# A table that overrides single decisions of a list scheduler, in an attention and feed-forward kernel

## The chip, the cores and the metric

The kernel runs on one core of a Trainium2 chip. The metric is device time in microseconds (us), the median of several runs. Before the change it is 757.0 us, the median of three (756.21, 757.00, 758.24). The profile shown is of one execution with a span of 754.6 us.

## The reference

One transformer block on x of 2048 rows and 512 columns, bf16: a layer norm, attention with 32 heads of width 16 and no mask, a residual, a second layer norm, and a gated feed-forward block of width 1792.

```python
qkv = layernorm(x) @ wqkv                    # 32 heads, Dh = 16
scores = einsum("bhqd,bhkd->bhqk", q, k) * 16 ** -0.5
h = x + einsum("bhqk,bhkd->bhqd", softmax(scores), v) @ wo
n = layernorm(h)
out = h + (sigmoid(n @ w_gate) * (n @ w_up)) @ w_down
```

The size that matters is the number of exponentials: 32 heads of 2048 x 2048 scores, 134 million.

## The kernel before, in words

**Units and rounds.** The work on the scores is cut into units. A unit is 128 keys by 512 queries of one head, or 256 keys by 256 queries in two halves; either way it fills one bank of PSUM, the matmul accumulator memory, as 128 x 512. Units go in *rounds*, numbered from 0, 695 of them. A round takes two or, for most of the kernel, three units. TensorE (PE) writes their scores (line 1085). ScalarE (ACT) takes the exponential of two or three neighbouring units in a single instruction (line 1408) and writes it as fp16 to *slots* in SBUF, the on-chip memory. The last unit of a round can go to VectorE (DVE) instead: a *split*. There the exponential is approximated by a sum of three pieces: VectorE makes an integer word (line 1256, tile J), GpSimd (POOL) makes two shifted copies of it by 64-bit additions (line 1277), and all three are multiplied with the values. So a unit on VectorE needs three value matmuls where a unit on ScalarE needs one. GpSimd or VectorE work is done for two such units at a time, and six buffers hold those pairs.

**Value rows.** Line 1233 multiplies the exponentials with V, augmented by a column that sums them. The output of a head has only 17 rows, so four heads (the strips j = 0 to 3 of a group) share the PE array side by side: four units, one from each strip, form a *row*. A slot is free again only when its unit's value matmul is done. A group's sum stays in PSUM until VectorE has moved it out (line 1151, tile xs); a later group that uses the same part of the accumulator waits for that.

**Dense steps.** Everything else that PE does (projections, the output projection, the feed-forward matmuls of lines 824 and 842) is a queue of background steps of two or so 512-column matmuls, called `bg`. A pace of *tokens* per round spreads them over the rounds. The feed-forward work of the last query block, which needs the end of attention, stands behind the last round as a tail.

**The planner.** The order on every engine is decided while the program is built, and written out as a fixed order. A planner keeps a clock for each engine in the dictionary T (P for PE, A for ScalarE, D for VectorE, G for GpSimd), with constant costs: `MM = 216.0` ns for a 512-column matmul or a value row, `SWITCH = 112.0` ns when PE changes between scores, value rows and dense work, `51 + 426.5 * wa` ns for the exponential of `wa` units, 601 ns for a unit on VectorE. In each round n it

- emits the scores of round n+1 (choosing its units in `pick`, line 1027; `st["dj"]` names the strip whose unit goes to VectorE),
- decides whether round n is split (`split`, from line 1395): VectorE must be near enough in time and a pair buffer free,
- finds neighbouring free slots (`p_slots`, line 1342); if there are none, it emits value rows until there are, and ScalarE has to wait for those,
- emits the exponential, and
- fills PE's time until that exponential is over (the loop `while T["P"] < lim - 100`, from line 1425): a dense step if the tokens and the room allow it, else up to three full value rows, else a warming matmul, else it moves PE's clock on by 100 ns and looks again.

All of these are compile-time choices. On the chip the engines work through their fixed lists and wait for each other by semaphores alone. A decision in one round changes which units, slots and steps all the later rounds find.

Of the kernel before, what the change touches and what calls it, by code (L numbers as in the profile page):

```python
# [18 lines left out]
DependencyInfo = mybir.DependencyInfo  # L19
DependencyClass = mybir.DependencyClass  # L20
DependencyReason = mybir.DependencyReason

LOG2E = 1.4426950408889634

# [118 lines left out]
def kernel(  # L143
# [12 lines left out]
    P = 128  # L156
# [318 lines left out]
    left = {n for n, t in tasks.items() if t.end is None}  # L475
# [121 lines left out]
    def run_dve(until, slack=450.0):  # L597
        while T["D"] < until:
            first = None
            for job in dq:  # L600
                r = job.ready()
                if r is None:
                    continue
                if r <= T["D"] + 60 and T["D"] + job.ns <= until + slack:
                    break
                first = r if first is None else min(first, r)
            else:
                if chain and T["D"] + chain[0][0] <= until + slack:
                    pop_chain()
                    continue  # L610
                if first is not None and T["D"] < first < until:
                    T["D"] = first
                    continue
                return
            dq.remove(job)
            job.place("D")
# [19 lines left out]
    MM = 216.0  # L636
# [312 lines left out]
    def ready_bg(i):  # L949
        while i < len(bg) and bg[i][2] is None:  # L950
            advance(i)
        if i >= len(bg):
            return None
        ns, mm, deps = bg[i][2]
        deps = [d() if callable(d) else d for d in deps]
        ends = [d.end for d in deps if d is not None]
        return None if None in ends else max(ends, default=-LAT) + LAT

    def try_bg(tokens, loose=60.0, depth=1):
        owner = next((i for i, item in enumerate(bg) if item is st["open"]), None)  # L960
        for i in range(depth) if owner is None else (owner,):
            r = ready_bg(i)
            if i >= len(bg):
                return 0
            if r is not None and r <= T["P"] + loose:
                break
        else:
            return 0
        ns, mm, deps = bg[i][2]
        if tokens < mm:  # L970
            return 0
        T["P"] = max(T["P"], r)
        pe_time("dense", ns)
        st["mark"] = Mark(T["P"] + DRAIN)
        advance(i)
        return mm
# [50 lines left out]
    def pick(want):  # L1027

        out, used = [], set()
        last = None  # L1030
        b = blocks[0]
        if want:
            j = st["dj"] % 4
            if b.a[j]:
                last = (b.qc, b.g, b.a[j].popleft(), j)
                st["dj"] = j + 1
                used.add(j)
        while blocks and len(out) + (last is not None) < wide["n"]:
            b = blocks[0]
            js = [j for j in range(4) if b.a[j]]  # L1040
            if not js:
                blocks.popleft()
                used.clear()
                if last is not None:
                    used.add(last[3])
                continue
            j = max(js, key=lambda j: (j not in used, len(b.a[j]), -((j - st["aj"]) % 4)))
            out.append((b.qc, b.g, b.a[j].popleft(), j))
            st["aj"] = j + 1
            used.add(j)  # L1050
        while blocks and not blocks[0].left():
            blocks.popleft()
        return out + ([last] if last is not None else [])
# [194 lines left out]
    half = []  # L1248
# [126 lines left out]
    while n + 1 < len(tiles):  # L1375
        n += 1
        tl = tiles[n]
        st["n"] = n
        early_on = any(b[1][0] in EARLY for b in bg)
        if st["R"] > 1 and wide["i"] == 0 and late(st["R"] - 1):  # L1380
            while st["open"] is not None:
                flush()
                try_bg(1e9, 1e12)
            for job in st["pms"][-3:]:
                place_now(job)
            st["R"] -= 1
            wide["base"], wide["n"] = PLACES[st["R"]][0]
            N = n + 2 + -(-sum(b.left() for b in blocks) // GU)
        if blocks:
            pss_n[n + 1] = scores(n + 1)  # L1390
        pss = pss_n.pop(n)
        start = max(T["A"], sc_end[n] + LAT)
        busy = sum(j.ns for j in dq if j.ready() is not None) + sum(c[0] for c in chain)
        dable = len(tl) > 1 and busy <= 1500
        split = (dable and max(T["D"], sc_end[n] + LAT) <= start + 600 and bool(half or len(quads) < QB))
        if n > N - 12:
            end = max(T["D"], sc_end[n] + LAT) + 1900 + 600 * (GQ - len(half[1:]) if half else GQ)
            split = split and end <= start + 1330 * (N - n) - 500
        if half and half[1][0].u[:2] != tl[-1][:2]:
            dexp_rest()  # L1400
            quads[:] = [q for q in quads if any(un in avq for un in q)]
            split = split and len(quads) < QB
        wa = len(tl) - split
        more_slots()
        free_at, row = p_slots(wa)
        pt = row[0].tile[:, row[0].i:row[0].i + wa, :]
        start = max(T["A"], sc_end[n] + LAT, free_at + LAT)
        ex = nc.scalar.activation(out=pt, in_=pss[:, 0:wa, :], func=ACT.Exp, scale=AS)  # L1408
        T["A"] = start + 51 + 426.5 * wa
        ex_end[n] = T["A"] + TAIL["A"]  # L1410
        for ui, u in enumerate(tl[:wa]):
            row[ui].unit = Unit(u, pt[:, ui, :], n, ex_end[n], row[ui])
            avq.append(row[ui].unit)
        if split:
            dexp_first(pss[:, wa, :], tl[-1], n)
            ex_end[n] = max(ex_end[n], T["D"] + TAIL["D"])
        run_act()
        if early_on:
            rate = 8.0
        else:  # L1420
            rate = max((st["left"] + st["todo"]) / max(N - 2 - n, 1), st["left"] / (PREP - n) if n < PREP else 0.7)
        tokens = min(tokens + rate, 8.0)
        hor = max(T["A"], sc_end.get(n + 1, 0.0) + LAT)
        lim = ex_end[n] + LAT
        while T["P"] < lim - 100:
            run_dve(min(T["P"], hor))

            def room(mode):
                return lim + OVER - T["P"] - (0 if st["mode"] == mode else SWITCH)
            if early_on or room("dense") >= (bg[0][2][0] if ready_bg(0) is not None else 2 * MM):  # L1430
                used = try_bg(tokens, depth=3 if early_on else 2)
                if used:
                    tokens -= used
                    st["left"] -= used
                    continue
            fit = int(room("av") // MM) * 4
            uns = av_ready(60.0)
            last = 0 < len(uns) == av_last()
            if fit >= 4 and av(min(12, fit), full=not last):
                continue  # L1440
            if quiet() and room("dense") >= MM and stir():
                continue
            T["P"] += 100
        run_dve(hor)
        if tl[0][0] == NCH - 1 and tiles[n - 1][0][0] == NCH - 2:
            nc.sync.dma_start(out=xl[:, 0:CW[NCH - 1] // P, :], in_=x_v[:, CQ[NCH - 1] // P:NT, :])
        if fw is None and After(("q", 0, NP - 1)).end is not None:
            spare[:] = [item for item in spare if not item[2]]
            while any(s.early and s.unit in avq for s in slots):
                flush()  # L1450
                if av(8, 1e12):
                    continue
                if half:
                    dexp_rest()
                if chain:
                    pop_chain()
            slots[:] = [s for s in slots if not s.early]
            pre.close()
            fw = main.enter_context(tc.tile_pool(name="fw", bufs=1, reuse_waits="tile"))
            fpool = main.enter_context(tc.tile_pool(name="fpool", bufs=1, reuse_waits="tile"))  # L1460
            fwork = main.enter_context(tc.tile_pool(name="fwork", bufs=1, reuse_waits="tile"))
            wd = fw.tile([P, FC, D], BF16, name="wd")
            nc.sync.dma_start(out=wd[:], in_=B_w_down.rearrange("(f p) n -> p f n", p=P))
            GW.extend(load_gate(f) for f in (0, 2))
# [149 lines left out]
```

## Time and profile before

| What | Before |
|---|---|
| device time, median of three | 757.0 us |
| span of the profiled execution | 754.6 us |
| PE busy | 718.8 us (95%) |
| ScalarE busy | 709.2 us (94%) |
| VectorE busy | 621.7 us (82%) |
| GpSimd busy | 396.0 us (52%) |
| first exponential starts, last one ends | 13.1 us, 718.6 us |
| exponentials on ScalarE of 2 units, of 3 units, of 1 unit | 636, 49, 10 |
| units on VectorE (J of line 1256) | 619 |
| tail behind the last exponential | 36 us |

"Busy" is the time in which at least one instruction of the engine is open in the profile. Instructions overlap: a matmul or an exponential is shown from when it starts until its results are written, while the next one is already running. The distance from one start to the next is the better measure of what an instruction costs its engine, and the prediction uses it.

### The profile page before, as it was taken

Reading aid. Unit: us, or ns where it says so; the run is one execution under the profiler, and the core shown is the slowest. Engines: PE = TensorE matmul, PEld = TensorE weight load, DVE = VectorE, ACT = ScalarE, POOL = GpSimd, SP = SyncE. Lnnn points to the kernel's source line nnn. Section 1 sums busy time; section 2 is a strip of 40 time slices with the busy share of each in tenths; the row PEclk is TensorE's granted clock in tenths of the full one; section 3 lists DMA queues with packets and bytes.
Section 4 is the critical chain, followed back from the end, with each engine's and each line's share of the span. In section 5 each row is a group of like instructions: output and inputs, shape, how many; then the busy total and the mean of one; then the engine's idle time right before and its main releaser. Section 6 shows DMA issues by size and latency. Waiting matters only on the chain.

```text
span 754.6 us, 27232 instructions
## 1 busy us (share of the span) xinstructions
PE 718.8 (95%) x11541; PEld 347.4 (46%) x11617; DVE 621.7 (82%) x1231; ACT 709.2 (94%) x788; POOL 396.0 (52%) x709
## 2 busy tenths in 40 slices
PE   7999998889999999999999999999999999999997
PEld 3322224444454445444555454535544455445554
DVE  7988878889978898898889688977889777899743
ACT  7989989999999999999999999999999999899952
POOL 2733546666556456655645546564555446465600
PEclk9999999999999999999999999999999999999999
DMA  7000005000123003210222122201321133003160
GB/s 238 1 1 1 1 18 153 2 3 3 30 87 99 10 10 109 78 30 10 78 59 59 36 79 58 74 22 38 99 59 30 44 93 107 10 9 105 47 203 17
DMA packets 68927, 41.65 MB, mean 55 GB/s; under 512 B 3520, under 2 KB 68800, under 8 KB 68800
## 3 DMA queue, kind: packets, MB, share of 16 engines
q1 hardware_dynamic: 68512, 39.59, 17.9%
q8 instruction: 92, 1.51, 0.9%
q14 instruction: 35, 0.29, 0.1%
q10 hardware_dynamic: 288, 0.26, 0.1%
HBM read 37.75 MB, written 2.10 MB: 53 GB/s over the span
## 4 chain that ended last, share of the span: by engine, by line
PE 74%; ACT 13%; DVE 8%; issue 4%; DMA 0%; POOL 0%; DVEq 0%; ACTq 0%; POOLq 0%
PE PS L1085 24%; PE PS L1233 23%; PE PS L824 14%; ACT pt L1408 10%; PE PS L842 6%; DVE J L1256 4%; PE PS L311 2%; PE PS L316 2%; PE PS L763 1%; ACT QTb L1408 1%; DVE xs L1151 1%; ACT xnT L1408 1%; PE PS L1560 1%; DVE st L271 1%; PE PS L305 1%
## 5 line engine op out<-in xcount | busy, mean ns | idle before, releaser
L1277 POOL INT64_ADD J<-J x640 | 377.6, 603 | 305.3 <-DVE J L1256 261.4
L1408 ACT ACTIVATE pt<-PS 128x1024 f16<-128x1024 f32 (+2 forms) x517 | 517.3, 1104 | 13.3 <-PE PS L1085 5.1
L1256 DVE TENSOR_SCALAR J<-PS 128x512 int16<-128x512 f32 x619 | 413.8, 681 | 70.1 <-PE PS L1085 42.7
L1085 PE MATMUL PS<-QT,KT 32*128 32x256 bf16 (+1 forms) x3712 | 263.8, 276 | 10.9 <-ACT pt L1408 4.9
L1233 PE MATMUL PS<-J,Vaug 128*17 128x256 f16 (+1 forms) x3546 | 243.4, 279 | 3.3 <-DVE xs L1151 1.9
L1233 PE MATMUL PS<-pt,Vaug 128*17 128x256 f16 (+1 forms) x2043 | 205.0, 279 | 2.8 <-DVE xs L1151 2.3
L1233 PEld LDWEIGHTS <-Vaug 128*17 128x17 bf16 x6204 | 139.3, 90 | 91.5 <-issue 84.4
L1085 PEld LDWEIGHTS <-KT 32*128 32x128 bf16 x3840 | 89.1, 92 | 197.2 <-issue 193.8
L824 PE MATMUL PS<-xnT,wgu 128*128 128x256 bf16 x784 | 113.7, 275 | 0.1
L1408 ACT ACTIVATE xnT<-PS 128x1024 f16<-128x1024 f32 x90 | 95.0, 1080 | 0.9 <-PE PS L1085 0.7
L824 PEld LDWEIGHTS <-wgu 128*128 128x128 bf16 x784 | 63.6, 97 | 39.6 <-issue 34.2
L1233 PE MATMUL PS<-xnT,Vaug 128*17 128x256 f16 x362 | 56.4, 274 | 0.0
L842 PE MATMUL PS<-wd,hT 128*128 128x512 bf16 x169 | 51.2, 383 | 2.5 <-issue 2.5
L1151 DVE STREAM_TRANSPOSE xs<-PS 128x256 f32<-128x256 f32 (+1 forms) x60 | 27.7, 461 | 21.9 <-PE PS L1233 21.2
L854 ACT ACTIVATE th<-PS 128x512 f32<-128x512 f32 (+1 forms) x63 | 37.4, 594 | 8.4 <-DVE hT L837 6.7
L1408 ACT ACTIVATE QTb<-PS 128x1024 f16<-128x1024 f32 x40 | 42.7, 1068 | 0.5 <-PE PS L1085 0.5
L896 DVE SCALAR_TENSOR_TENSOR hT<-th,PS 128x512 bf16<-128x512 f32 x49 | 33.3, 680 | 7.3 <-PE PS L824 7.2
L1233 PE MATMUL PS<-QTb,Vaug 128*17 128x256 f16 (+1 forms) x158 | 28.4, 275 | 0.0
L1408 ACT ACTIVATE xb<-PS 128x1024 f16<-128x1024 f32 (+2 forms) x26 | 25.6, 1030 | 2.1 <-PE PS L1085 1.1
L1122 DVE TENSOR_TENSOR o<-xs,rsum 128x128 bf16<-128x128 f32 (+1 forms) x60 | 24.4, 407 | 2.1
L1408 ACT ACTIVATE pe<-PS 128x1024 f16<-128x1024 f32 (+2 forms) x22 | 21.7, 1062 | 1.7 <-PE PS L1233 1.4
L842 PEld LDWEIGHTS <-hT 128*128 128x128 bf16 x196 | 12.2, 97 | 20.8 <-issue 17.8
(128 smaller groups left out, 397.5 us busy)
## 6 DMA issues: line engine op xcount, KB each, us to landing
wgu<-in_B_w_gate_dram SPq DMA_DIRECT2D x49, 256.0 KB, 3.0
wgu<-in_B_w_up_dram SPq DMA_DIRECT2D x49, 256.0 KB, 3.5
out_dram<-ob SPq DMA_DIRECT2D x16, 128.0 KB, 2.1
wd<-in_B_w_down_dram SPq DMA_DIRECT2D x1, 1792.0 KB, 8.8
xr<-in_A_x_dram SPq DMA_DIRECT2D x14, 128.0 KB, 3.8
xb<-in_A_x_dram SPq DMA_DIRECT2D x6, 256.0 KB, 6.0
J<-in_B_w_gate_dram SPq DMA_DIRECT2D x4, 384.0 KB, 5.9
J<-in_B_w_up_dram SPq DMA_DIRECT2D x4, 384.0 KB, 7.0
```

What stands on the lines that cost most here:

```text
L311: nc.tensor.matmul(ps, lhsT=w_sb[:, d, p * P:(p + 1) * P], rhs=xnT[c][:, d, :], start=(d == 0), stop=(d == DC - 1))
L824: nc.tensor.matmul(ps[:, 0:PARTS[r][2]], lhsT=w[:, d, :], rhs=hn_of(r)[:, d, :], start=(d == 0), stop=(d == DC - 1))
L842: nc.tensor.matmul(ps, lhsT=hT[:, f, i * P:(i + 1) * P], rhs=wd[:, f, :], start=(f == 0), stop=(f == FC - 1))
L854: nc.scalar.activation(out=th[:, 0:ps.shape[-1]], in_=ps, func=ACT.Tanh, scale=0.5)
L896: nc.vector.scalar_tensor_tensor(out=hT[:, f:f + k, 0:w], in0=th[f][:].rearrange("p (k n) -> p k n", k=k), scalar=1.0, in1=ps2.rearrange(" ...
L1085: nc.tensor.matmul(pss[:, ui, i * CW[qc]:(i + 1) * CW[qc]], lhsT=KT[g // 2][32 * j:32 * j + 32, k * P:(k + 1) * P], rhs=q[32 * j:32 * j + ...
L1122: nc.vector.tensor_tensor(out=o2[:, 0:w // 32, DH * a:DH * a + DH], in0=xs[:, 0:w // 32, 0:DH], in1=rec.to_broadcast([P, w // 32, DH]), op ...
L1151: j = dve(650 - ns[0], lambda: nc.vector.transpose(out=xs[:, 0:w // 32, :].rearrange("p b r -> p (b r)"), in_=src), Mark(T["P"] + DRAIN), ...
L1233: nc.tensor.matmul(dst[32 * j:32 * j + VW, 0:w], lhsT=un.v[:, kt * SPAN[qc] + i, h, :], rhs=un.ap[:, i * w:(i + 1) * w], start=clears and ...
L1256: nc.vector.tensor_scalar(out=J[:, 0, k, :], in0=src, scalar1=ZOFF, scalar2=float(-min(CHORDS)), op0=ALU.add, op1=ALU.max)
L1277: nc.gpsimd.int64_add(words(s), words(0), CHORDS[s - 1] * (1 + 2 ** 16 + 2 ** 32 + 2 ** 48))
L1408: ex = nc.scalar.activation(out=pt, in_=pss[:, 0:wa, :], func=ACT.Exp, scale=AS)
```

## The change

A dictionary `PLAN` is added, with 92 entries. The key is 16 times the round plus a place in it. Places 0, 1, 2 are the first passes of the filling loop; place 15 is the split; place 14 is the strip for VectorE. The table was found by a search on a model of the clocks of the engines; its purpose is to replace the planner's rule in rounds in which another choice lets the model end earlier. The rules themselves and all constants stay as they are.

What an entry says, and how many there are:

| Place | Value | Meaning | Entries |
|---|---|---|---|
| 0 to 2 | 1, 2, 3 | up to that many value rows now, not necessarily full ones | 10, 11, 17 |
| 0 to 2 | 4 | a dense step now, whatever the tokens say | 17 |
| 0 to 2 | 5 | nothing: PE's planned clock moves on by 100 ns | 7 |
| 0 to 2 | 9 | leave the filling of this round | 7 |
| 15 | 1 | no split in this round | 8 |
| 15 | 2 | a split, whatever the rule says of time (a pair buffer must be free) | 7 |
| 14 | 1, 2, 3 | another strip's unit goes to VectorE | 1, 5, 2 |

```diff
+PLAN = {414: 2, 528: 5, 656: 5, 672: 2, 736: 4, 737: 3, 750: 2, 769: 9, 801: 2, 815: 1, 817: 2, 1198: 3, 1200: 3, 1201: 3, 1376: 1, 1409: 3, 1423: 1, 1472: 9, 1473: 5, 1474: 4, 1601: 9, 1634: 3, 1682: 4, 1696: 9, 1713: 4, 1840: 9, 1857: 5, 1872: 4, 1873: 1, 1890: 9, 1938: 1, 2033: 1, 2047: 1, 2144: 5, 2145: 2, 2161: 2, 2384: 2, 2417: 4, 3728: 3, 3730: 4, 4240: 1, 4255: 1, 4321: 3, 4353: 4, 4367: 2, 4752: 2, 4753: 5, 4767: 2, 6112: 5, 6129: 3, 7040: 3, 7041: 3, 7696: 4, 7711: 1, 7713: 4, 7742: 2, 7761: 9, 7904: 2, 8512: 4, 8513: 3, 8913: 1, 8926: 3, 8928: 2, 8930: 1, 8943: 2, 8944: 4, 8960: 3, 8975: 1, 9200: 3, 9393: 4, 9410: 4, 9889: 4, 9890: 3, 9952: 2, 9984: 3, 10000: 2, 10178: 3, 10302: 2, 10528: 3, 10543: 2, 10640: 1, 10687: 2, 10703: 2, 10848: 4, 10894: 2, 10945: 1, 10959: 2, 11023: 1, 11089: 4, 11102: 1, 11103: 1, 11106: 1}
...
-            j = st["dj"] % 4
+            j = (st["dj"] + PLAN.get(16 * len(tiles) + 14, 0)) % 4
...
         split = (dable and max(T["D"], sc_end[n] + LAT) <= start + 600 and bool(half or len(quads) < QB))
+        alt = PLAN.get(16 * n + 15, 0)
+        if alt == 1:
+            split = False
+        elif alt == 2:
+            split = len(tl) > 1 and bool(half or len(quads) < QB)
...
+        step = 0
         while T["P"] < lim - 100:
             run_dve(min(T["P"], hor))
+            alt = PLAN.get(16 * n + step, 0)
+            step += 1
 
             def room(mode):
                 return lim + OVER - T["P"] - (0 if st["mode"] == mode else SWITCH)
+            fit = int(room("av") // MM) * 4
+            if alt == 9:
+                break
+            if alt == 5:
+                T["P"] += 100
+                continue
+            if 0 < alt < 4 and fit >= 4 and av(min(4 * alt, fit)):
+                continue
+            if alt == 4:
+                used = try_bg(8.0, depth=2)
+                if used:
+                    tokens -= used
+                    st["left"] -= used
+                    continue
```

The first entry is in round 25 and the last in round 694. Between them they stand thick in rounds 25 to 51 (11 entries), 84 to 155 (24), 480 to 559 (14) and 560 to 694 (26), thin from 156 to 479 (14), with 3 more in rounds 52 to 83.

## The prediction

> **What bounds the kernel now.** I first read the busy times on the page, to see which engines can be the bound at all.
>
> ```profile
> PE 718.8 (95%) x11541; PEld 347.4 (46%) x11617; DVE 621.7 (82%) x1231; ACT 709.2 (94%) x788; POOL 396.0 (52%) x709
> ...
> ACT  7989989999999999999999999999999999899952
> ...
> PEclk9999999999999999999999999999999999999999
> ```
>
> PE and ScalarE are both at 94 to 95%, and busy time can't separate them, since it counts overlapped latency. So next I read the groups by form and a piece of the timeline in which two exponentials stand together.
>
> ```profile
> L1408 ACT ACTIVATE pt<-PS 128x1024 f16<-128x1024 f32 x468 | 455.7, 1075 | 5.3 <-PE PS L1085 3.7 <-PE PS L1233 0.2
> ...
> L1408 ACT ACTIVATE pt<-PS 128x1536 f16<-128x1536 f32 x44 | 64.6, 1477 | 7.9 <-issue 4.1 <-PE PS L1233 2.1 <-PE PS L1085 1.3
> ```
>
> ```profile
> 348.86 1.94 ACT L1408 ACTIVATE pt<-PS 128x1024 f16<-128x1024 f32 x2
> ```
>
> One exponential of two units lasts 1.02 to 1.08 us, yet two take 1.94: the second starts some 0.90 us after the first. From the start times of all of them, the pitch of two-unit exponentials is 904 ns at the tenth percentile and 905 in the middle, of three-unit ones 1331, of the tanh of 512 columns 478, of one-unit ones 477. ScalarE's real work from the first exponential (13.1) to the last one's end (718.6) is therefore 636 x 904 + 49 x 1331 + 10 x 477 + 49 x 478 = 574.9 + 65.2 + 4.8 + 23.4 = 668.3 us of 705.5. **ScalarE is idle for 37.2 us there**, 5%. Of that 28.2 us lies in 70 gaps of over 150 ns, the rest is jitter of some 15 ns a round.
>
> For PE I did the same: a run of scores (216 ns of columns) is followed by the next kind of work after 330 to 333 ns in over half the cases, so changing the kind costs 115 ns. Value rows cost 340, 558, 776 ns for one, two, three rows (218 a row), and a dense step 543. Against such prices PE has about 10% of its time free from 168 us on, and 30% from 117 to 168. So **ScalarE is the bound**, PE is close behind, and what is left to gain inside the fixed work is ScalarE's gaps. The largest one:
>
> ```profile
> 640.04 1.49 ACT L1408 ACTIVATE pt<-PS 128x1536 f16<-128x1536 f32 x1
> ...
> 643.13 0.45 DVE L1151 STREAM_TRANSPOSE xs<-PS 128x256 f32<-128x256 f32 x1 [3.33 <-PE PS L1233]
> ...
> 643.63 0.28 PE L1233 MATMUL PS<-pt,Vaug 128*17 128x256 f16 x2 [0.57 <-DVE xs L1151]
> ...
> 644.32 1.45 ACT L1408 ACTIVATE pt<-PS 128x1536 f16<-128x1536 f32 x1 [2.79 <-issue]
> ```
>
> The scores of the exponential at 644.32 were done long before (the last score matmuls ahead of it on PE ended at 642.07). What it waited for was three neighbouring free slots: the old units could be multiplied only after VectorE had emptied the accumulator at 643.6. The waits of ScalarE add up the same way:
>
> ```profile
> ACT pt L1408 <- PE PS L1085: 5.1, 13, 1.5
> ...
> ACT pt L1408 <- issue: 4.1, 2, 2.8
> ACT pt L1408 <- PE PS L1233: 2.3, 3, 1.1
> ```
>
> Late scores (L1085) are many small waits. Value rows that free slots (L1233, and the two called "issue") are few and long.
>
> **What the Trainium skill says.** "Perfetto Trace Analysis", Optimizing Scalar/DVE Operations: an instruction's fixed cost is about 51 ns for ScalarE on PSUM, and the profiled latency is longer because the write-acknowledgement overlaps the next instruction. The trace agrees: 904 pitch against 1075 duration, and 1331 - 904 = 427 a unit leaves 904 - 2 x 427 = 50 ns. The same page, Identifying the Most-Contended Engine, says that matmul busy time is no measure of how near PE is to its limit; here 95% busy goes with some 10% of free pitch. "TensorEngine Tiling (Array Packing)", Key Properties: changing the tiling mode drains the engine. The 115 ns above is that price here.
>
> **The change, part by part.** No entry adds arithmetic except through splits; the units, scores and dense matmuls stay.
>
> *Splits.* An enforced no-split turns a 904 exponential into a 1331 one: +427 ns on ScalarE; it takes 601 ns from VectorE, and from PE two of three value units, 2 x 55 = 110 ns (a row of four is 218). A forced split is the reverse. If all eight and all seven change the rule's choice: +8 x 427 - 7 x 427 = +0.4 us on ScalarE. The ends are +3.4 (only the eight bite) and -3.0 us. I take +0.4. The 49 three-unit exponentials show that forced splits find rounds to bite on.
>
> *Value rows* (38 entries). They move rows, they add none. A block cut out of another costs PE up to one more change, 115 ns, and a row that isn't full wastes up to 218 x 3/4 = 164. Ends: 0 and 38 x 279 = 10.6 us of PE, over 660 us in which PE has some 60 free. I take 38 x 115 x one half = 2.2 us, hidden by that free time. What it buys is slots freed a round earlier.
>
> *Dense steps* (17). Each is a step of 543 ns taken earlier; the tokens go down and later rounds give it back. Zero on PE's sum. Scores queued behind it on PE come 0.54 us later at worst, and the exponential behind those waits only if less than that was in hand.
>
> *Leaving the round* (7) and *the 100 ns of nothing* (7). No instruction. The first lets PE reach the next round's scores earlier, which is what an exponential waiting on L1085 needs; the work left out comes later. *Other strip* (8): no cost in itself; it changes how full later rows are.
>
> Head and tail: nothing stands before round 25, so the first 36 us of the trace must stay. Of dense work the tail holds 25 down matmuls by the records (a few are missing), and by the code one reserved block of 28 stays for it, so it can only stay or grow. So only **ScalarE's gaps from round 25 on** can pay: 28.2 - 2.0 (before round 25) = 26.2 us. By stage, gaps over 150 ns: rounds 25 to 51, 5.4 us; 84 to 99, 2.9; 230 to 259, 3.4; 330 to 429, 4.6; 480 to 559, 2.3; 560 to 619, 4.0; the others together 3.6. The gaps that begin in or within a dozen rounds after an entry are (from my list of gaps) 4.0 us in 35 to 52, 2.9 in 84 to 95, 0.9 in 236 to 308, 1.2 in 494 to 544, 0.9 in 561 to 592, 2.9 in 619, 0.7 in 673 to 687: 13.5 us. An entry stands in round 92, just ahead of the gap of 1.66 us in front of round 94's exponential, in 494 ahead of 0.90, in 618 ahead of 2.95. I take it that half of the 13.5 goes: 6.8 us. Not all of it, because a slot that comes earlier needs PE time, and the accumulator's emptying on VectorE (about 1 us with its waits) is not moved. The other 12.7 us of gaps are thrown anew, since every later round finds other units; I take no change on the mean. Net of splits: -6.8 + 0.4 = -6.4; rounded for what the jitter eats of it, **-6 us: 751.0**.
>
> Does a plan made on clocks hold on the chip? The constants in the code are 904 and 1330.5 for ScalarE, where the trace has 904 and 1331; 328 for scores and a change, where it has 330; 540 for a dense step, where it has 543; for three full rows 3 x 216 + 12 x 4 + 112 = 808, where it has 776. The long gaps, slot and accumulator waits, have their rule in the planner. So shifts of a microsecond should carry over; shifts of 50 ns may not.
>
> **Rivals.**
> (1) *The gaps only move.* ScalarE's gaps are of the schedule's kind (slots run short at the ends of groups), and removing one lets ScalarE run on to the next shortage. For it: 18 of the entries lie in rounds 100 to 155, where ScalarE loses only 0.9 us, so they can't pay where they stand. Against: most gaps lie in the rounds with the other entries. Time: 757.
> (2) *Slower.* All eight no-splits bite (+3.4 us), four of the forced splits do (-1.7), and ScalarE meets one new shortage of slots of the size of the one at round 337 (1.2 us). For it: the 38 entries of value rows take rows that the rule held back until they were full, and 92 departures are many. Against: PE's free time. Time: 757 + 2.9 = 759.9. A background step pushed behind the last round would add 0.43 us more each.
> (3) *Much more.* The later gaps shrink too, 12 of the 26.2 us go, and forced splits save 2 more: 757 - 14 = 743. Against: each long gap would have to go without a successor.
>
> **How the numbers follow.** Forecast, 747 to 754: 0.59. Rival 1: 0.15. Rival 2: 0.16. Rival 3: 0.10. The predicted time is the likeliest, 751.0. The range, 745.5 to 758.5, takes in the forecast, rival 1 and the split's ends on either side (751 - 3.0 - 2 to 757 + 1.5), and leaves most of rivals 2 and 3 out, 2 in 10. A bound of 0.3% is 2.3 us: faster means below 754.7. Of the forecast nearly all is, with rival 3: 0.69. Same: 0.16. Slower: 0.15.
>
> **What would show it.** Right: the last exponential starts some 6 us earlier, with the head to 36 us and the tail (36 us) as they are; the count of three-unit exponentials stays at 49 give or take 5; the waits of ScalarE on "issue" and L1233 shrink, the 2.79 us wait near 644 above all. Wrong: the same sum of gaps in other rounds (rival 1); more three-unit exponentials, or a longer tail with more dense matmuls in it (rival 2). The prediction fails if the planner's clocks leave out a wait that the new order runs into.

## The result and the profile after

The changed kernel takes 751.58 us (median of four, 750.73 to 752.46) against 757.62 us for the kernel before on the same chip (four runs, 756.21 to 758.48). The ratio is 0.9924, with a 95% interval of 0.9906 to 0.9941: faster by 6.0 us. The profiled span is 749.0 us against 754.6.

The first lines of the page after, which answer to those of before (busy us, share of the span, instructions):

```profile
PE 714.2 (95%) x11497; PEld 346.0 (46%) x11571; DVE 617.5 (82%) x1223; ACT 710.6 (95%) x788; POOL 392.4 (52%) x715
...
ACT  8988999999999999999999999999999999999952
```

The shares say nothing: they are the same to a point. The number of VectorE instructions has gone down by eight. What became of ScalarE is seen in its groups by form (line, names, shapes, count | busy us, mean ns of one | idle us before it, and what ended it):

```profile
L1415 ACT ACTIVATE pt<-PS 128x1024 f16<-128x1024 f32 x466 | 457.8, 1085 | 6.7 <-PE PS L1087 3.3 <-PE PS L1235 3.0
...
L1415 ACT ACTIVATE pt<-PS 128x1536 f16<-128x1536 f32 x46 | 68.7, 1509 | 2.3 <-PE PS L1235 1.8 <-PE PS L1087 0.4
```

The three-unit exponentials of this group waited 7.9 us before and wait 2.3 now (all lines have moved by some numbers: 1415 is the exponential, 1235 the value rows, 1087 the scores). With the pitches of the prediction, which are the same in both kernels, the span comes apart into four terms; the gaps are what the other three leave over:

| us | before | after | difference |
|---|---|---|---|
| up to the first exponential | 13.12 | 13.06 | -0.06 |
| ScalarE's work, first to last exponential | 668.36 | 671.77 | +3.42 |
| ScalarE's gaps in the same stretch | 37.17 | 29.84 | -7.33 |
| tail behind the last exponential | 35.91 | 34.33 | -1.59 |
| span | 754.56 | 749.00 | -5.56 |

The work term is 8 x 427 ns: eight units fewer on VectorE (611 against 619), 56 three-unit exponentials against 49. The waits of ScalarE, read like those of before:

```profile
ACT pt L1415 <- PE PS L1235: 4.8, 5, 1.8
...
ACT pt L1415 <- PE PS L1087: 3.8, 13, 0.7
```

The two waits on "issue", 4.1 us together, are gone, among them the one of 2.79 us in front of the exponential at 644.32. In the timeline after, the same stage of the kernel runs through (start, length, engine, what):

```profile
635.42 6.05 ACT L1415 ACTIVATE pt<-PS 128x1024 f16<-128x1024 f32 x6
...
639.14 0.27 PE L1235 MATMUL PS<-pt,Vaug 128*17 128x256 f16 x1
...
640.26 0.44 DVE L1153 STREAM_TRANSPOSE xs<-PS 128x256 f32<-128x256 f32 x1
```

Six exponentials stand in one unbroken piece, while PE finishes a group's value rows and VectorE empties the accumulator beside them. So far the gaps are as forecast; the last exponential ends 4.0 us earlier (714.7 against 718.6 us), where some 6 us had been forecast. Where the gaps went is another matter. ScalarE's gaps by stage (a gap counts for the round that it follows), and the entries of the table that stand there:

| rounds | entries | before | after |
|---|---|---|---|
| 0-24 | 0 | 2.1 | 2.1 |
| 25-51 | 11 | 5.7 | 6.4 |
| 52-99 | 9 | 3.9 | 3.1 |
| 100-229 | 18 | 2.3 | 3.0 |
| 230-329 | 10 | 6.0 | 5.9 |
| 330-429 | 2 | 6.6 | 3.6 |
| 430-559 | 16 | 3.7 | 2.7 |
| 560-619 | 7 | 5.0 | 1.2 |
| 620-694 | 19 | 1.7 | 1.6 |

The 38 entries up to round 155 stand in stages where the gaps grew by 0.5 us in all (12.6 to 13.1 up to round 155). The greatest savings, 3.0 and 3.8 us, are in stages with two and seven entries. Nor does every entry do something. The planner's program, run on the table with each entry struck out in turn, writes the same order as with the full table in 45 of the 92 cases, and also when all 45 are struck out together: 24 stand at a pass that the filling loop doesn't reach in that round, 7 are the forced splits, and the others change nothing where they stand. So the column counts orders given, and 47 of them shape the kernel.

### The profile page after: what moved, and what is told of

It is laid out like the page before. It is cut to its first block, busy times and chain, and to the rows that moved or that the text cites. A ratio compares the mean times of both kernels' runs of the same rounds, so it can differ in the third digit from the quotient of the medians.

```text
span 749.0 us, 27149 instructions
## 1 busy us (share of the span) xinstructions
PE 714.2 (95%) x11497; PEld 346.0 (46%) x11571; DVE 617.5 (82%) x1223; ACT 710.6 (95%) x788; POOL 392.4 (52%) x715
## 4 chain that ended last, share of the span: by engine, by line
PE 71%; ACT 18%; DVE 6%; issue 4%; DMA 0%; POOL 0%; DVEq 0%; ACTq 0%; POOLq 0%
PE PS L1087 24%; PE PS L1235 22%; PE PS L826 13%; ACT pt L1415 12%; PE PS L844 5%; DVE J L1258 3%; PE PS L318 2%; ACT xnT L1415 2%; PE PS L765 2%; PE PS L313 2%; ACT pe L1415 1%; DVE xs L1153 1%; PE PS L1584 1%; ACT xb L1415 1%; ACT th L856 1%
## 5 line engine op out<-in xcount | busy, mean ns | idle before, releaser
L1415 ACT ACTIVATE pt<-PS 128x1024 f16<-128x1024 f32 (+1 forms) x516 | 520.8, 1119 | 9.2 <-PE PS L1235 4.8
L1258 DVE TENSOR_SCALAR J<-PS 128x512 int16<-128x512 f32 x611 | 408.4, 681 | 76.6 <-PE PS L1087 43.4
L1087 PE MATMUL PS<-QT,KT 32*128 32x256 bf16 (+1 forms) x3712 | 263.7, 276 | 13.6 <-ACT pt L1415 8.0
L1235 PE MATMUL PS<-J,Vaug 128*17 128x256 f16 (+1 forms) x3486 | 238.2, 279 | 2.0 <-DVE xs L1153 1.1
L1235 PE MATMUL PS<-pt,Vaug 128*17 128x256 f16 (+1 forms) x2049 | 195.6, 279 | 1.3 <-DVE xs L1153 1.0
L1087 PEld LDWEIGHTS <-KT 32*128 32x128 bf16 x3840 | 88.6, 92 | 197.7 <-issue 193.8
L1235 PEld LDWEIGHTS <-Vaug 128*17 128x17 bf16 x6164 | 138.4, 90 | 88.2 <-issue 82.5
L1415 ACT ACTIVATE xnT<-PS 128x1024 f16<-128x1024 f32 (+1 forms) x89 | 97.8, 1128 | 0.2
L826 PEld LDWEIGHTS <-wgu 128*128 128x128 bf16 x784 | 63.8, 98 | 38.9 <-issue 33.6
L1235 PE MATMUL PS<-xnT,Vaug 128*17 128x256 f16 x368 | 54.4, 273 | 0.0
L1415 ACT ACTIVATE QTb<-PS 128x1024 f16<-128x1024 f32 x42 | 45.8, 1090 | 0.6 <-PE PS L1087 0.6
L1235 PE MATMUL PS<-QTb,Vaug 128*17 128x256 f16 (+1 forms) x166 | 27.5, 275 | 0.4 <-DVE xs L1153 0.4
```

The source lines that it names most:

```text
L826: nc.tensor.matmul(ps[:, 0:PARTS[r][2]], lhsT=w[:, d, :], rhs=hn_of(r)[:, d, :], start=(d == 0), stop=(d == DC - 1))
L1087: nc.tensor.matmul(pss[:, ui, i * CW[qc]:(i + 1) * CW[qc]], lhsT=KT[g // 2][32 * j:32 * j + 32, k * P:(k + 1) * P], rhs=q[32 * j:32 * j + ...
L1235: nc.tensor.matmul(dst[32 * j:32 * j + VW, 0:w], lhsT=un.v[:, kt * SPAN[qc] + i, h, :], rhs=un.ap[:, i * w:(i + 1) * w], start=clears and ...
L1258: nc.vector.tensor_scalar(out=J[:, 0, k, :], in0=src, scalar1=ZOFF, scalar2=float(-min(CHORDS)), op0=ALU.add, op1=ALU.max)
```

## The experiments

Two theories. **One path:** an entry has no worth of its own. It changes what every later round finds, and the table is good as a whole, because the course to which it leads happens to be a short one. What tells how good a table is would then be the planner's own clock at the end; the planner is part of the kernel's program and gives that clock for any table. **Each entry where it stands:** the reading of the prediction, in which entries take away the gaps next to them, so that parts of the table give parts of the gain.

### The first 38 entries alone

```diff
-PLAN = {414: 2, ..., 2417: 4, 3728: 3, ..., 11106: 1}
+PLAN = {414: 2, ..., 2417: 4}
```

> Only the 38 entries of rounds 25 to 155; from round 156 on the rule decides everything, on the state that the table leaves. Theory one path (what counts is the whole course, and the chip follows the planner's own end clock): the planner's PE clock at the last value row is 705.2 against 708.9 without a table and 702.5 with the full one, so -3.7 us: about 753.9 us if before is 757.6; 51 three-unit exponentials. Up to round 155 ScalarE's gaps are as in the changed kernel, after it gaps of slots come back at other places. Rival, each entry works where it stands: gaps of the rounds to 155 fell by only 1.6 us in the changed kernel, so about 756 us.

Measured: 753.43 us against 756.68, ratio 0.9956 (0.9939 to 0.9972), that is -3.3 us; 51 three-unit exponentials. When round 156 starts, this kernel is only 0.9 us ahead of the one before (167.55 against 168.43 us from the start of the span); when round 430 starts, it is 3.9 us ahead (444.01 against 447.88), further than the kernel with the full table (445.83). Rounds 330 to 429, where it has no entry, have 2.7 us of gaps instead of 6.6, and rounds 560 to 619 1.8 instead of 5.0; in rounds 620 to 694 some come back, 3.8 instead of 1.7. Most of what these entries save, they save hundreds of rounds later. The rival's 756 us is outside the interval. Its reason doesn't hold either: the 1.6 us in the expectation are the gaps of rounds 84 to 99 alone, while over all rounds to 155 the gaps grew, as the table above shows. The 0.9 us come from ScalarE's work, which is 1.3 us less up to there (ten three-unit exponentials instead of fourteen).

### One entry less

```diff
-PLAN = {..., 1198: 3, 1200: 3, 1201: 3, ...}
+PLAN = {..., 1198: 3, 1201: 3, ...}
```

> The full table less one entry, that of round 75, place 0 (three value rows). Theory one path: all rounds after 75 are decided anew on a state for which the other entries were not chosen; the planner's end clock is 714.1, 5.1 us over the kernel before: about 762.7 us, slower than before. Rival, each entry works where it stands: one of 92 entries is worth about 6/92 = 0.07 us, the time stays at about 751.6.

Measured: 760.97 us against 756.68, ratio 1.0056 (1.0040 to 1.0073). 91 of the 92 entries are 4.3 us slower than none, and about 10 us slower than all. ScalarE's work is that of the changed kernel (671.8 us, 56 three-unit exponentials); the gaps are 40.2 us instead of 29.8, more than before. The list of its ScalarE waits shows the same two kinds as before the change, late scores (L1087) and value rows that free slots (L1235):

```profile
ACT pt L1415 <- PE PS L1087: 6.9, 19, 2.4
...
ACT pt L1415 <- PE PS L1235: 6.5, 5, 1.8
```

The sums, 6.9 and 6.5 us, are to be read against 3.8 and 4.8 us of the changed kernel. The longest that the changed kernel doesn't have stand behind rounds 94 (2.6 us), 237, 333, 480 and 618, all after the missing entry. For this entry that refutes the second theory: losing it costs some 10 us and not 0.07, and 8.5 of the 10.4 us of added gaps lie in rounds 430 to 694, far behind it. It is not a typical entry, though. By the planner's clock it is among the three of the 92 whose loss costs most (9.8 us, the highest being 10.4), 45 cost nothing, and without the one of round 694 at place 2 the clock would even end 1.5 us earlier. Only this one and one of round 693, below, were struck out on the chip.

### The same entries in other rounds

```diff
-PLAN = {414: 2, 528: 5, 656: 5, ..., 11106: 1}
+PLAN = {479: 1, 625: 1, 706: 1, ...}
```

> The same 92 values at the same places of a round, but in rounds drawn at random from 25 to 694. Theory one path: a random departure from the rule gives an ordinary course; 200 such tables have a planner's end clock of 714.4 on the mean, standard deviation 2.1, the least 709.1; this one has 714.8, so +5.9 us: about 763.5 us, with 60 three-unit exponentials against 49. Rival, the kinds of choice themselves help (more value rows and dense steps early): about 752 to 757.

Measured: 763.23 us against 756.68, ratio 1.0084 (1.0068 to 1.0101), +6.6 us; 60 three-unit exponentials, gaps of 39.1 us. The kinds of choice do not help by themselves. This arbitrary course is 6.6 us worse than the one that the rule takes, and by the planner's PE clock so are all 200 (the least 709.1 against 708.9). Busy shares don't tell it from the others. The first line of its page:

```profile
PE 723.7 (95%) x11495; PEld 347.0 (46%) x11571; DVE 614.8 (81%) x1219; ACT 717.4 (94%) x788; POOL 389.1 (51%) x705
```

It is 12 us slower than the changed kernel, with 95 and 94% as before the change. Nor is it short of slots. Its waits for value rows (L1235 and "issue") are 3.4 us, against 6.4 in the kernel before; the late scores are 6.0 against 5.1:

```profile
ACT pt L1415 <- PE PS L1087: 6.0, 16, 1.1
...
ACT pt L1415 <- PE PS L1235: 2.3, 3, 1.4
...
ACT pt L1415 <- issue: 1.1, 1, 1.1
```

### Without the entries on splits

```diff
-PLAN = {..., 750: 2, ..., 815: 1, 817: 2, ...}
+PLAN = {..., 750: 2, ..., 817: 2, ...}
```

(815 and the fourteen others with place 15 are struck out.)

> The table without its 15 entries on splits, 77 are left. Theory one path: planner's end clock 709.3 against 708.9 before, so about 758 us, no gain; 46 three-unit exponentials. Rival of the prediction's sum (the ordering entries remove ScalarE's gaps, the splits cost a little): the gaps of the changed kernel stay away and the splits' 3 us of ScalarE work is saved as well, so about 749 us.

Measured: 760.15 us against 756.68, ratio 1.0050 (1.0033 to 1.0067), +3.5 us; 46 three-unit exponentials, work 667.5 us, gaps 41.0 us. The rival is refuted by 11 us: the entries on splits can't be taken out of the table to save their 3.4 us. But the first theory is off too, by 3 us, the most in this study. Against the planner's clocks this kernel's exponentials fall behind by 2.0 us in rounds 330 to 430 and by another 1.3 us up to round 560, with the largest single step at the gap before round 557: 2.5 us where the planner has 1.8. Why just here stays open.

### Two tables from a longer search

```diff
-PLAN = {414: 2, 528: 5, 656: 5, 672: 2, ...}
+PLAN = {414: 2, 528: 5, 656: 5, 671: 1, 672: 2, 720: 2, 750: 2, 815: 1, 1200: 3, 1216: 3, 1248: 1, 1343: 1, 1376: 2, 1392: 1, 1423: 1, 1568: 9, 1857: 9, 1873: 1, 1936: 2, 2047: 1, 2161: 3, 2210: 9, 2320: 9, 2384: 2, 3728: 3, 4240: 1, 4255: 1, 4353: 4, 4416: 3, 4752: 3, 6112: 5, 6576: 3, 7040: 3, 7711: 1, 7742: 2, 7904: 2, 8513: 2, 8928: 2, 8960: 3, 8975: 1, 9200: 3, 9296: 2, 9376: 2, 9393: 4, 9712: 2, 9728: 2, 9952: 2, 9984: 3, 10000: 2, 10302: 2, 10528: 3, 10640: 1, 11023: 1, 11089: 4, 11103: 1, 11104: 1, 11106: 1}
```

> Another table of 57 entries, found by going on from the table of the changed kernel: single entries added, altered or struck out at random, and kept when the planner's own clock of VectorE after the last group came earlier. It stands at 701.1 against 704.3 for the changed kernel and 710.7 for the kernel before. Theory one path: 3.2 us below the changed kernel if all of it holds, about 748.5 us when before is 757; 57 three-unit exponentials, ScalarE's gaps some 3 us less. Rival, the clocks have been used up (what is left are errors of the planner's constants that a longer search exploits): no faster than the changed kernel, 751 to 753.

> A second such table, from another random course (40 of its 57 entries are those of the changed kernel), with the planner's clock at 702.0, 2.2 us below the changed kernel: about 749.4 us. Rival as for the first: 751 to 753.

> The changed kernel itself, on the chip of these runs, so that the two longer searches can be set against it: 0.9924 of the kernel before, about 751.5 us.

Measured: 747.45 us, ratio 0.9878 (0.9863 to 0.9893), for the first; 748.98 us, 0.9896 (0.9881 to 0.9911), for the second (edit not shown: 57 entries of the same kinds, 40 of them those of the changed kernel); 750.69 us, 0.9921 (0.9907 to 0.9934), for the changed kernel; all against 756.66 us. So -3.2 and -1.7 us below the changed kernel, where 3.2 and 2.2 had been expected. So what the longer search gained on the planner's clock was not mainly its errors. The first is the fastest version of the study, 9.2 us below the kernel before. Its terms: work 672.6 us (57 three-unit exponentials), gaps 27.0, tail 32.8.

### One late entry alone, and the table without it

```diff
-PLAN = {414: 2, 528: 5, ..., 11106: 1}
+PLAN = {11103: 1}
```

The second kernel is the changed one with only `11103: 1` struck out.

> The kernel before with a single entry: no split in round 693, the last but one. Nothing follows that it could upset. Theory on the tail (a unit on VectorE so late keeps PE waiting for its three value rows, behind the last exponential): ScalarE's work +0.43 us, one more three-unit exponential (50), but the last value row comes earlier and the tail is 1.5 to 1.9 us shorter; in all -1.4 us, about 755.4 us. Rival (more work for ScalarE, the bound, costs what it weighs; the tail has a fixed length): +0.4 us, about 757.2.

> The changed kernel without that same entry. If an entry had a worth of its own, taking it out would cost 1.4 us: about 752.5 us. Theory one path: in this course it is not needed; the planner's clock differs by 0.2 us, so 751.0 as the changed kernel (0.992 of before), with 55 three-unit exponentials.

Measured: 754.75 us against 757.19 with the single entry, ratio 0.9972 (0.9960 to 0.9983), -2.4 us; 751.26 us without it, 0.9925 (0.9912 to 0.9939). One entry, where nothing follows that it could upset, has a worth of its own, two fifths of what the whole table gives (interval 1.3 to 3.0 us; the profiled spans differ by 1.9), and in the whole table it gives nothing. Before the change the end of the timeline reads:

```profile
718.66 1.28 ACT L1480 ACT_TABLE_LOAD   x1
...
720.39 1.46 PE L1485 MATMUL PS<-wo_sb,ot 128*128 128x512 bf16 x6
721.77 0.39 PE L1233 MATMUL PS<-J,Vaug 128*17 128x256 f16 x4
```

With the single entry:

```profile
719.05 1.28 ACT L1504 ACT_TABLE_LOAD   x1
...
720.02 0.38 PE L1235 MATMUL PS<-pt,Vaug 128*17 128x256 f16 x2
...
720.77 1.46 PE L1509 MATMUL PS<-wo_sb,ot 128*128 128x512 bf16 x6
```

The table load marks the end of the last exponential. It comes 0.4 us later (719.05 against 718.66): the unit that ScalarE now does. But before, a last block of value rows, those of VectorE's words (J) first, stood behind six matmuls of the output projection, until 722.4 us; now all rows are done at 720.4, ahead of that projection. From the last exponential's end to the end of the last value row are 3.7 us before, 1.4 with the entry, 2.2 in the changed kernel, 2.4 in it without the entry, and 0.6 in the fastest version; from there to the end of the span it is 32.1 to 32.4 us in all five.

## Why the prediction was right, and where it was not

The total was met, but in part by luck: the splits cost 3.0 us more than forecast, and the tail (1.6 us) and the gaps (0.5 us) gave back most of that.

**The bound: ScalarE's share was read rightly, PE's was not.** ScalarE's 668 us of work and 37 us of gaps stand. The step that failed is "Against such prices PE has about 10% of its time free from 168 us on". PE's time was taken apart for this into blocks of one kind (scores, value rows, dense work), by the starts of its weight loads in the traces; what each block holds is known from the planner's program. At the pitches that most blocks of a size have (332 ns for scores; 336, 555 and 773 for one, two and three rows; 538 for a dense step, all at or a few ns below the prediction's), from the first scores to the last:

| | before | changed kernel | one entry less | other rounds | longer search |
|---|---|---|---|---|---|
| blocks on PE | 1422 | 1398 | 1408 | 1437 | 1400 |
| PE's work, us | 677.2 | 672.6 | 680.8 | 682.9 | 673.0 |
| PE's idle time, us | 26.9 | 27.2 | 29.1 | 28.4 | 24.8 |

From 168 us on, PE of the kernel before is idle for 14.4 of 549 us, 2.6%, while ScalarE's gaps there are 4.5%. So PE was the fuller engine in most of the kernel. By what the profile infers, late scores end 45 of the 69 gaps of over 150 ns between ScalarE's instructions, 15.5 us in all; value rows and "issue" end 12, 10.1 us. After the change these are 12.4 and 7.3 us, so both kinds have shrunk.

The prediction gave PE extra changes of kind (38 x 115 x one half = 2.2 us). It has fewer instead: 24 blocks less, at 115 ns each, are 2.8 us. (That these 115 ns are the price of a drain, as the prediction reads them, no run here shows.) In the changed kernel the last scores come 4.4 us earlier because PE has 4.6 us less to do, not because it waits less. The longer search wins on idle time too; the two slower tables shown lose on both, and the one without the entries on splits on idle time alone (30.3 us). No run changes the number of blocks alone, so whether fewer blocks make the short course or come along with it stays open.

**Gaps: -6.8 us forecast, -7.3 measured.** The size was right and the reason for it wrong. The step that failed is "The gaps that begin in or within a dozen rounds after an entry ... I take it that half of the 13.5 goes", together with "The other 12.7 us of gaps are thrown anew ... I take no change on the mean". Over the first 155 rounds the gaps grew, though those of rounds 84 to 99 fell by 1.7 us; the most was saved far away, and the runs with 38 and with 91 entries show that the effect of an entry needn't be where it stands. That half of 13.5 came out near the true sum was luck. (By its own rule the sum also leaves out the gaps behind rounds 25 to 33, just after the first entry, 1.7 us.) The gap before round 620, to which the prediction tied an entry of round 618, is gone already in the kernel that has no entry after round 155: all rounds from 560 to 619 together have 1.8 us of gaps there. And the two entries of round 618 are among those that the planner's loop doesn't reach.

**Splits: +0.4 us forecast, +3.4 measured,** the upper end of what was given. All eight orders not to split took effect; of the seven forced splits none did: the planner's rule had chosen the split in those rounds anyway, in the course that the table makes. To set both kinds off against each other was the error, and with 56 three-unit exponentials the count left the 49 give or take 5 that the prediction had named as a sign of being right. That eight orders gave just eight units isn't a rule: without the 15 entries on splits the table ends at 46, not at 49. An order that repeats the rule costs and gains nothing, and a table grown by trial can carry such leftovers.

**Tail: "it can only stay or grow" forecast, -1.6 us measured.** The count of dense matmuls was watched, and not the value rows behind the last exponential. Their end, not the dense steps, sets when the tail proper can start: it is the part behind them that stays at 32 us, and the single late entry takes 2.3 us off the rest (tail 33.6 against 35.9 us).

**The planner's clocks hold on the chip**, as the prediction argued from the constants. In ten kernels the exponentials start within -1.4 and +4.1 us of the planner's times over some 700 us, once the first is set equal. The gain of a table against the kernel before, by the planner's clock of VectorE after the last group and as measured (us):

| kernel | planner | measured |
|---|---|---|
| changed kernel | -6.4 | -6.0 |
| first 38 entries | -3.7 | -3.3 |
| one entry less | +3.4 | +4.3 |
| other rounds | +4.2 | +6.6 |
| no entries on splits | +0.4 | +3.5 |
| longer search | -9.6 | -9.2 |
| second longer search | -8.6 | -7.7 |
| single late entry | -1.5 | -2.4 |
| table without it | -6.6 | -5.9 |

(The expectations of the first four experiments used PE's clock. Its differences are up to 1.7 us off these, and for the single late entry it has +0.3 where -2.4 was measured.) By VectorE's clock, which the longer searches used, the order is right throughout, but for the changed kernel and the table without the late entry, which were measured 0.1 us apart. For the tables that no search had chosen the clock is too kind by 0.9 to 3.1 us where they are slower than none.

**Rivals.** That the gaps only move (757) and that the change is slower (760) were both wrong for this table, though of the second one sign came true, more three-unit exponentials. A table next to it is slower: 91 entries give 761. Much more than 6 us (743) is not reached by the best table found, 747.5.

## What to carry to other kernels

Where a fixed order is made by a list scheduler whose clocks agree with the trace to some microseconds in 700, a search over its choices, judged by its own end clock, can carry over to the chip nearly in full (three tables here: 6.0 of 6.4 us, 9.2 of 9.6, 7.7 of 8.6), and it needs no chip to run. Such a table is one course and not a sum of improvements: one entry less cost all of the gain and more, while another could go for nothing. So after a change of a size or a constant it should be searched anew; how much of it would survive was not measured. Strike out the entries that change nothing, to see what the table does. When two engines are both 95% busy, take the distance from start to start of the instructions, multiply by the counts, and split the span into work, gaps and tail; those three terms told apart kernels whose busy shares were equal. Do it for both engines: PE's sum, which the prediction had at 10% free, shows why ScalarE waited.

## What was not expected of the hardware

With 695 exponentials and some eleven thousand matmuls in fixed orders, the chip repeats most of the planned gaps themselves: the gaps of over 1 us in the traces of six kernels stand in the same rounds as the planner's, mostly within 0.4 us of its length (1.66 us where it has 1.86 in round 94 of the kernel before, 2.59 where it has 2.57 in round 95 with one entry less). The largest departures are 2.95 against 2.29, before the change in front of round 620, 0.99 against 2.06 without the entries on splits in front of round 98, and 1.19 against 0.39 with the entries in other rounds in front of round 326. Shorter gaps are less sure: 0.90 us before round 495 of the kernel before are not in the plan, and 0.93 us planned ahead of round 98 of the changed kernel did not come. ScalarE's pitch did not move: 904 ns before and 903 or 904 ns after for two units, 1331 and 1330 for three.
